# Recurrent attention and a feed-forward layer on one core: token pairs for the logits, sums on row halves, and another order of work

## Chip, cores and metric

The kernel runs on one core of a Trainium2 chip. The metric is device time in microseconds; the table below gives the runs of the kernel before the change, their median and the one execution that was profiled.

## What is computed

The reference is a gated recurrence over 768 tokens for 4 x 8 heads of width 48, and a feed-forward layer on its output:

```python
f = 1.0 / (1.0 + np.exp(-f_logit))                  # B, H, S, D = 4, 8, 768, 48
for t in range(S):
    state = f[:, :, t, :, None] * state + np.einsum('bhd,bhe->bhde', k[:, :, t], v[:, :, t])
    y[:, :, t] = np.einsum('bhd,bhde->bhe', q[:, :, t], state)
x = y.transpose(0, 2, 1, 3).reshape(B * S, H * D)    # 3072 x 384
h = x @ w_in                                         # 384 x 2048
out = (h * (1.0 / (1.0 + np.exp(-h)))) @ w_out       # 2048 x 384
```

Inputs and output are float32 in DRAM; the matmuls work on bf16 operands.

## The kernel before

The 768 tokens of each of the 4 batches are cut into 6 chunks of 128. A work item is a pair of two chunks, and `PAIRS` lists 12. Pairs 0 to 3 (form T) hold chunks 0 and 1 of one batch, with two neighbouring tokens in one partition, so their loads read 384 bytes in one run (two tokens of 48 floats). Pairs 4 to 11 (form N) hold the same chunk of two batches, one token per partition, so their loads read 192 bytes in one run.

For each pair the logits `f` become softplus values `lf` on ScalarE (`E` an Exp, line 312, `L` a Ln, lines 324 and 327). TensorE sums them over the tokens with a triangular matrix (`cs`, lines 388 and 395), and gives in a few columns more the total of a chunk (lines 392 and 398). ScalarE takes Exp of the sums (`a`, `ia`, `al`, lines 400, 402, 342). VectorE and GpSimd multiply q and k with them (`qg`, `ki`, line 405). q and k are turned either on TensorE with a copy out of PSUM (`tq`, line 412, `qkc`) or by a DMA transpose on SP's queue (`qkD`, line 424). Then come the scores (`sc`, lines 434 and 438, on the array's row halves because a head has 48 rows), the mask (`at`, line 442), y (`y`, `yi`, lines 349, 455, 459), the state (`d`, `sd`, `su`, lines 361, 476, 480, 490), and y turned into `xT` (`yT` on TensorE, line 467, with a copy `xc`, or `yD` by DMA, line 471).

The feed-forward layer works per pair in 8 tiles of hidden columns: `mi` (line 335, x times w_in, six matmuls of 256 columns, or two halves of 128 columns for pairs 0 and 1), `si` (line 340, Silu on ScalarE). The second product takes the plain form for pairs 0, 1 and 11 (`mo`, line 370) and for the others one that saves an eighth of the multiplications by summing halves of the hidden values (`hs`, line 256) and of w_out (`wt`, line 246) on VectorE: seven products `ms` (line 273), combined by `cc`, `ca` and `oc` before the store `so`.

The order on every engine is written out by hand in the table `PLAN`. A word such as `cs.4.1:P:3` names the operation, the pair and half, the engine (P TensorE, A ScalarE, V VectorE, G GpSimd, S SP's DMA queue) and the buffer it takes. Each engine runs its words in the order of the table and waits by semaphore for what they need. Loads of q, k, v and f go through SP's queue. The weights go through GpSimd's queue (`wi`, line 237, `wo`, line 240), which casts them to bf16 on the way, so their issue stands in line with GpSimd's products. `idle` (line 545) issues matmuls on a cleared tile, whose result nobody reads. ScalarE changes its function table (line 593) whenever it goes from Exp and Ln to Silu or back.

Of the kernel before, what the change touches and what calls it, by code (L numbers as in the profile page):

```python
# [11 lines left out]
BF16 = mybir.dt.bfloat16  # L12
AF = mybir.ActivationFunctionType
ALU = mybir.AluOpType
# [23 lines left out]
PLAN = """  # L38
f.1.0:S:0 k.1.0:S:0 f.0.0:S:1 f.0.1:S: q.1.0:S:0 f.2.0:S:2 E.1.0:A: L.1.0:A:0 v.1.0:S:0 cs.1.0:P:0 E.0.0:A: q.0.0:S:1 L.0.0:A:1 idle.512.1::1
cs.1.1:P:1 a.1.0:A:0 E.0.1:A: k.0.0:S:1 qg.1.0:V:0 L.0.1:A: a.1.1:A:1 f.3.0:S:0 ia.1.1:A:2 idle.512.2::2 cs.0.0:P:2 qg.1.1:V:1 ia.1.0:A:3 ki.1.1:G:  # L40
cs.0.1:P:3 al.1:A:0 E.2.0:A: q.2.0:S:2 ki.1.0:V: ia.0.0:A:4 tq.1.0:P:4 vb.1.0:V:0 a.0.0:A:0 v.0.0:S:1 vb.1.1:A:1 qkc.1.0:V:0 qg.0.0:G:2 a.0.1:A:1
d.1:P:5,6 L.2.0:A:2 k.2.0:S:2 tq.1.1:P:7 su.1.0:V:0 qg.0.1:G:3 qkc.1.1:A: cs.2.0:P:0 ki.0.0:V: k.3.0:S:3 wi.3:G: sd.1.1:V:0 ia.0.1:A:2 sc.1.0:P:1,2
# [12 lines left out]
mo.1.0.2:P: vb.3.1:V:2 q.4.1:S:4 sd.2.1:V:1 yi.2.1:P: sc.3.1:P:3,6 yc.2.1:V:2 su.2.1:G:0 q.4.0:S: sc.3.0:P:7,4 mo.0.0.3:P: E.4.0:A: at.3.0.0:V:0
k.5.0:S:0 mo.1.0.3:P: at.3.1.0:V:1 L.4.0:A:1 yT.2.0:P:5 at.3.1.1:V: yT.2.1:P:7 v.4.0:S:4 mo.1.1.3:P: xc.2.1:A:2 at.3.0.1:V: oc.1.0:A:0 cs.4.1:P:3
v.5.0:S:0 cs.4.0:P:6 xc.2.0:V: oc.1.1:A: oc.0.0:V:1 d.3:P:7,4 a.4.1:A:1 y.3:P:0,5 q.5.0:S:0 su.3.0:V:0 al.4.1:A:4 ia.4.0:A:4 qg.4.1:G:3 mi.2.7:P:2
E.5.0:A: yc.3.0:V:0 v.6.1:S:1 mi.2.3:P:1 ia.4.1:A:2 sd.3.1:V:0 al.4.0:A:5 yi.3.1:P: a.4.0:A:3 yT.3.0:P:7 f.7.0:S:0 mi.2.1:P:0 su.3.1:G:0 L.5.0:A:2
xc.3.0:V:3 yc.3.1:V:1 mi.2.4:P:3 v.4.1:S: wt.4:V: yT.3.1:P:4 cs.5.0:P:6 mi.2.0:P:7 xc.3.1:V: ki.4.1:V: mi.2.5:P:5 si.2.0:A:2 vb.4.0:V:3 qkD.4.1:S:0
ki.4.0:V:0 mi.2.2:P:4 si.2.7:A: qg.4.0:V: si.2.1:A: mi.3.7:P:7 wt.3:V: si.2.5:A: mi.3.2:P:2 qkD.4.0:S:1 si.2.4:A: si.3.7:A:3 d.4.0:P:0 mi.2.6:P:5  # L60
si.2.3:A: mi.3.1:P:3 si.2.6:A: mi.3.4:P:7 si.2.2:A: vb.5.0:A:0 mi.3.0:P:1 hs.2.1:V:2 q.6.0:S:1 si.3.2:A: vb.4.1:G:1 mo.0.1.0:P:5 si.3.4:A: k.7.0:S:1
wt.1:V: si.3.0:A: mi.3.5:P:4 sd.4.0:V:1 mi.3.6:P:2 f.6.0:S:1 si.3.5:A: wt.7:V: ms.2.3:P:7 si.3.6:A: q.5.1:S: hs.2.5:V:1 mi.3.3:P:1 si.3.1:A: d.4.1:P:0
cs.5.1:P:4 si.3.3:A: ms.2.4:P: sd.4.1:V:0 hs.2.7:V: k.6.1:S:2 sc.4.0:P:2,3 sc.4.1:P:1,0 at.4.0.0:V:2 mo.0.1.1:P: k.5.1:S: a.5.0:A:0 at.4.1.1:V:3
al.5.0:A:1 mo.0.1.2:P: al.5.1:A:0 ia.5.1:A:1 qg.5.0:G:4 at.4.1.0:V: q.6.1:S: ia.5.0:A:2 ms.3.3:P:2 E.7.0:A: cc.2:V:0 ki.5.0:G: at.4.0.1:V: y.4.1:P:0
f.8.0:S:2 L.7.0:A:0 ms.3.4:P: hs.2.6:V: yc.4.1:A:2 tq.5.0:P:6 k.6.0:S: a.5.1:A:4 y.4.0:P:1 qkc.5.0:V:3 E.6.0:A: mo.0.1.3:P: su.4.0:G:0 ca.2.0:V:
yT.4.1:P:3 yc.4.0:A:0 sc.5.0:P:0,4 v.6.0:S: L.6.0:A:1 su.4.1:G:0 d.5.0:P:6 ms.2.2:P: sd.5.0:V:1 q.7.0:S:2 yT.4.0:P:1 xc.4.1:V:0 qg.5.1:G:1 ms.2.5:P:
# [47 lines left out]
def kernel(  # L114
# [10 lines left out]
    nc = tc.nc  # L125
# [369 lines left out]
    def takes(kind, rest):  # L495
# [22 lines left out]
        if kind == "al":  # L518
            return [("al", *rest)]
# [107 lines left out]
```

## Time and profile before

| what | value |
| --- | --- |
| median of 3 runs | 177.3 us (176.36 to 177.46) |
| profiled execution, its own time | 175.56 us |
| its span, first to last instruction | 173.4 us |
| TensorE matmul busy | 160.4 us, 92% |
| ScalarE / VectorE / GpSimd busy | 75% / 70% / 41% |
| bytes moved by DMA | 31.73 MB, mean 183 GB/s |
| DMA packets | 108695, of which 102704 under 512 B |
| ScalarE table loads | 13 in the body, 16.7 us |

The profile is that of one execution. Its page gives busy time per engine, the span in 40 slices, the DMA queues, the chain of work that ended last, and the costliest groups of instructions by line; the trace behind it can be asked for stretches of time, single engines and single transfers. PE is TensorE's matmuls, PEld its weight loads, DVE VectorE, ACT ScalarE, POOL GpSimd, SP the engine that issues most DMAs (SPq and POOLq are the issues). A busy TensorE need not be at its peak, since ends of matmuls overlap, and idle time of an engine that nobody waits for costs nothing.

### The profile page before, as it was taken

To read this page: it belongs to the slowest core of one execution; us is meant where nothing else is said; L and a number is where in the kernel's file an instruction comes from. 1 tells how busy PE (TensorE), PEld (TensorE's weight loads), DVE (VectorE), ACT (ScalarE), POOL (GpSimd) and SP (SyncE) were. 2 spreads that over 40 slices of the span, in tenths; PEclk is the share of its full clock that TensorE was granted. 3 is DMA by queue.
4 is the path that set the end of the run, shared out by engine and by line. 5 is a ranking of instruction groups with operands and counts; after the bars stand their busy time and mean duration, and the time that the engine had idled before them with its cause. 6 is when DMAs were issued, how large, how long until landed. Compare 5 with 4: busy or idle time off the path is not lost.

```text
span 173.4 us, 5477 instructions
## 1 busy us (share of the span) xinstructions
PE 160.4 (92%) x2245; PEld 141.5 (82%) x2245; DVE 121.3 (70%) x234; ACT 129.6 (75%) x248; POOL 71.2 (41%) x115
## 2 busy tenths in 40 slices
PE   0687898999999999999999999999996999999993
PEld 0255698976789888999998999999895998999992
DVE  7188950039995997958899779989965677966050
ACT  3999697783989899999768798798955877603511
POOL 6059872930240147899946305202467201000300
PEclk9999999999999999999999999999999999999999
DMA  5999999999999999979999969896999795120305
GB/s 138 324 325 319 241 206 227 203 206 195 185 194 200 195 200 204 176 150 208 245 188 188 219 135 211 191 198 134 191 171 183 177 145 139 60 80 4 136 27 200
DMA packets 108695, 31.73 MB, mean 183 GB/s; under 512 B 102704, under 2 KB 108144, under 8 KB 108672
## 3 DMA queue, kind: packets, MB, share of 16 engines
q1 hardware_dynamic: 103936, 25.70, 71.7%
q0 software_dynamic: 4736, 5.70, 15.8%
q8 instruction: 17, 0.28, 0.6%
q14 instruction: 6, 0.05, 0.1%
HBM read 25.17 MB, written 4.72 MB: 172 GB/s over the span
## 4 chain that ended last, share of the span: by engine, by line
PE 69%; DMA 17%; POOL 4%; SPq 4%; ACT 3%; issue 1%; POOLq 0%
PE pb L335 28%; PE pb L273 22%; PE pb L370 7%; DMA w_in_sb<-in_moe_w_in_dram 6%; DMA w_out_sb<-in_moe_w_out_dram 5%; DMA qkT<-qk 4%; POOL qk L405 3%; DMA f<-in_f_logit_dram 2%; PE pb L438 2%; SPq L305 2%; PE pb L459 2%; PE pb L455 2%; PE pb L395 2%; SPq L424 1%; ACT x L400 1%
## 5 line engine op out<-in xcount | busy, mean ns | idle before, releaser
L335 PE MATMUL pb<-xT,w_in_sb 128*128 128x256 bf16 (+1 forms) x672 | 69.7, 257 | 0.5 <-DMA w_in_sb<-in_moe_w_in_dram 0.5
L340 ACT ACTIVATE hT<-pb 128x512 bf16<-128x512 f32 x96 | 51.9, 605 | 14.1 <-PE pb L335 13.4
L335 PEld LDWEIGHTS <-w_in_sb 128*128 128x128 bf16 x672 | 56.3, 98 | 5.9 <-DMA w_in_sb<-in_moe_w_in_dram 0.6
L273 PE MATMUL pb<-w_sum,hT 128*128 128x192 bf16 x288 | 28.0, 246 | 0.0
L405 POOL TENSOR_TENSOR qk<-q,x 128x384 bf16<-128x384 f32 x16 | 16.3, 1020 | 27.5 <-ACT x L400 12.4
L490 POOL TENSOR_TENSOR st<-sd,al 48x192 bf16<-48x192 f32 x32 | 16.9, 529 | 25.6 <-DVE sd L480 13.5
L400 ACT ACTIVATE x<-pb 128x384 f32<-128x384 f32 x48 | 22.2, 511 | 3.3 <-PE pb L395 2.7
L273 PEld LDWEIGHTS <-hT 128*128 128x128 bf16 x288 | 23.8, 98 | 0.6
L442 DVE TENSOR_TENSOR atm<-pb,triu 128x512 bf16<-128x512 f32 x32 | 20.5, 683 | 5.2 <-PE pb L438 5.0
L370 PE MATMUL pb<-w_out_sb,hT 128*128 128x384 bf16 (+1 forms) x128 | 17.7, 286 | 0.1
L593 ACT ACT_TABLE_LOAD x13 | 16.7, 1283 | 0.2
L405 POOL TENSOR_TENSOR qk<-k,x 128x384 bf16<-128x384 f32 x13 | 13.8, 1062 | 6.7 <-ACT x L400 5.4
L273 PE MATMUL pb<-w_out_sb,qkTT 128*128 128x192 bf16 x144 | 14.7, 246 | 0.0
L256 DVE TENSOR_TENSOR hT<-hT 128x1024 bf16<-128x1024 bf16 x18 | 14.6, 813 | 0.0
L382 POOL DMA_DIRECT2D out_dram<-ob x7 | 3.9, 565 | 24.6 <-ACT hT L340 24.6
L370 PEld LDWEIGHTS <-hT 128*128 128x128 bf16 x128 | 11.1, 98 | 3.6 <-issue 0.3
L191 ACT CAST yb<-pb 128x384 bf16<-128x384 f32 x15 | 7.3, 490 | 8.5 <-PE pb L349 4.8
L312 ACT ACTIVATE f<-f 128x768 f32<-128x768 f32 (+1 forms) x13 | 10.4, 809 | 2.4 <-DMA f<-in_f_logit_dram 2.2
L273 PEld LDWEIGHTS <-qkTT 128*128 128x128 bf16 x144 | 12.0, 98 | 0.3
L256 DVE TENSOR_TENSOR qkTT<-hT 128x2048 bf16<-128x2048 bf16 x9 | 11.1, 1233 | 1.2 <-ACT hT L340 1.2
L193 DVE COPY qkTT<-pb 128x1024 bf16<-128x1024 bf16 x4 | 2.8, 692 | 12.0 <-PE pb L412 12.0
L442 DVE TENSOR_TENSOR atm<-pb,mask 128x512 bf16<-128x512 f32 x16 | 10.0, 684 | 1.3 <-PE pb L434 1.3
(86 smaller groups left out, 235.6 us busy)
## 6 DMA issues: line engine op xcount, KB each, us to landing
f<-in_f_logit_dram SPq DMA_DIRECT2D x11, 384.0 KB, 4.8
k<-in_k_dram SPq DMA_DIRECT2D x16, 192.0 KB, 4.1
q<-in_q_dram SPq DMA_DIRECT2D x16, 192.0 KB, 3.7
v<-in_v_dram SPq DMA_DIRECT2D x16, 192.0 KB, 4.1
k<-in_k_dram SPq DMA_DIRECT2D x4, 384.0 KB, 4.9
q<-in_q_dram SPq DMA_DIRECT2D x4, 384.0 KB, 4.8
v<-in_v_dram SPq DMA_DIRECT2D x4, 384.0 KB, 10.7
w_in_sb<-in_moe_w_in_dram POOLq DMA_DIRECT2D x4, 384.0 KB, 8.8
```

The source lines that it names most:

```text
L191: nc.scalar.copy(dst, src)
L256: return ENG[eng].tensor_tensor(out=h_sum(P, m), in0=x, in1=y, op=op)
L273: nc.tensor.matmul(at(BANK[m], P)[:, half * W:(half + 1) * W], x, w, start=first, stop=(n == KH - 1), skip_group_check=True)
L312: return nc.scalar.activation(e, at("f", P)[:, j * w:(j + 1) * w], AF.Exp, scale=-1.0)
L335: nc.tensor.matmul(h[:, i, cols], w_in_sb[:, kk, n * 128:(n + 1) * 128], at("xT", P)[:, kk, cols], start=(kk == 0), stop=(kk == KT - 1))
L340: return nc.scalar.activation(at("hT", P).rearrange("p u n c -> p n u c")[:, 2 * j:2 * j + 2], at("h", P, j).rearrange("p (n u c) -> p n u ...
L370: nc.tensor.matmul(at("o", P, i)[:, cols], at("hT", P)[:, i, n], w_out_sb[:, n, cols], start=(n == 0), stop=(n == NT - 1))
L400: nc.scalar.activation(at(kind, P, i).rearrange("p h d -> p (h d)"), at("cs", P, i)[:, 0:HD], AF.Exp, scale=1.0 if kind == "ia" else -1.0)
L405: ENG[eng].tensor_mul(at("qk", P, i)[:, j, :, 0:D], heads("qk"[j], P, i), at("ia" if j else "a", P, i))
L442: ENG[eng].tensor_mul(at("atm", P, i)[:, r], at(f"s{r}", P, i).rearrange("p (n c) -> p n c", c=C), mask[:, None, :].to_broadcast([C, NP, C]))
L490: ENG[eng].tensor_mul(at("st", P, i)[lo:lo + D, :, r * D:(r + 1) * D], src[lo:lo + D, :, r * D:(r + 1) * D], al_of(P, i)[lo:lo + D, :, Non ...
L593: nc.scalar.preload_act_table_set(TABLES[mode])
```

## The change

Four things change. First, the logits of pairs 4 to 11 come as two neighbouring tokens per partition: each batch's chunk fills 64 partitions, in a DMA of its own with runs of 384 bytes. Second, their sums are made by one word `cs` per pair: for each parity of the token and each half of the partitions one matmul of 64 rows, with two new triangular masks `tpair`, and column sums on 64 rows likewise. Third, pair 0's logits come in one transfer with one Exp and one Ln instead of two. Fourth, `idle` reads the triangular mask repeated four times instead of a cleared tile, there are 7 such matmuls instead of 3, and the whole table has a new order: pair 0 goes ahead of pair 1, w_out is issued later, y of five more halves is turned by DMA (15 instead of 10 in form N), q and k of two halves fewer (12 instead of 14). The diff, without the table:

```diff
-    zero = sb.tile([C, 512], BF16, name="zero")
     two = any(kind == "T" for kind, *_ in PAIRS)
+    merged = {int(w.split(":")[0].split(".")[1]) for w in PLAN.split() if w.startswith("cs.") and w.split(":")[0].count(".") == 1}
+    if merged:
+        tpair = [sb.tile([C, C], BF16, name=f"tpair{j}") for j in range(2)]
...
-            if T:
+            if kind == "f" and P in merged:
+                for r in range(2):
+                    nc.sync.dma_start(out=at("f", P)[r * HC:(r + 1) * HC].rearrange("p (h w) -> p h w", h=H),
+                                      in_=f_logit[b + r, :, c * C:(c + 1) * C].rearrange("h (p t) d -> p h (t d)", t=2))
+                return
+            elif T:
...
-                if T:
+                if T or P in merged:
...
-            if T:
+            if T or P in merged:
...
+        if kind == "cs" and len(rest) == 1:
+            lf = at("lf", P)
+            for j in range(2):
+                for r in range(2):
+                    rows = slice(r * HC, (r + 1) * HC)
+                    nc.tensor.matmul(at("cs", P, r)[:, 0:HD].rearrange("p (h d) -> p h d", d=D), tpair[j][rows], lf[rows, j, :, 0:D], start=(j == 0), stop=(j == 1), skip_group_check=True)
+            if us[0][1] < CHUNKS - 1:
+                for j in range(2):
+                    for p in range(NP):
+                        for r in range(2):
+                            rows = slice(r * HC, (r + 1) * HC)
+                            nc.tensor.matmul(at("cs", P, r)[:, HD + p:HD + p + 1], lf[rows, j, 2 * p:2 * p + 2, :], ones[rows], start=False, stop=(j == 1), skip_group_check=True)
+            return
...
+        if kind == "cs" and len(rest) == 1:
+            return [(kind, P, i) for i in range(2)]
...
-                nc.tensor.matmul(buf["pb", int(got)][:, 0:rest[0]], triu, zero[:, 0:rest[0]], start=True, stop=True, skip_group_check=True)
+                nc.tensor.matmul(buf["pb", int(got)].rearrange("p (n c) -> p n c", c=C), triu, triu[:, None, :].to_broadcast([C, 4, C]), start=True, stop=True, skip_group_check=True)
...
-        nc.vector.memset(zero, 0.0)
...
+        if merged:
+            for j in range(2):
+                nc.gpsimd.memset(tpair[j], 0.0)
+                for r in range(2):
+                    half = tpair[j][r * HC:(r + 1) * HC]
+                    nc.gpsimd.affine_select(out=half, in_=half, compare_op=ALU.is_gt, fill=1.0, base=j, pattern=[[-1, C]], channel_multiplier=2)
```

Three places show how the table moves work. In each row stand the line, the operation, the tile written and the tiles read. The first place is TensorE's queue at the sums: before, pair 4's two halves stand between a product of `mo` and the state of pair 3.

```order
L395 MATMUL pb_135<-lf_80,triu 128x384
L398 LDWEIGHTS lf_80
L398 MATMUL pb_135<-ones,lf_80 128x1
...
L395 MATMUL pb_138<-lf_80,triu 128x384
...
L361 MATMUL pb_139<-vb_98,qk_89 128x96
```

Now, for pair 5, whose sums stand between the scores of pair 4's two halves (line 457, the old 438):

```order
L457 MATMUL pb_139<-qkT_99 128x128
...
L375 MATMUL pb_138<-lf_81,tpair_149 128x384
L375 LDWEIGHTS tpair_149
L375 MATMUL pb_136<-lf_81,tpair_149 128x384
...
L375 MATMUL pb_136<-lf_81,tpair_150 128x384
L381 LDWEIGHTS lf_81
L381 MATMUL pb_138<-ones,lf_81 128x1
...
L457 MATMUL pb_133<-qkT_100 128x128
```

What moved: two matmuls of 384 columns on full rows are four on row halves, in two PSUM banks in turn, and the sums now have scores, which are on row halves too, on both sides; for the other pairs of form N scores or other products on row halves stand on at least one side of the sums, or next to the sums of the pair beside them.

The second place is GpSimd's queue around the second weights. Before, they are issued after the state updates of pairs 0 and 1, between products of q and k (`qk`) of pair 3:

```order
L490 TENSOR_TENSOR st_140<-sd_122,al_124 48x4x48 x2
L490 TENSOR_TENSOR st_141<-sd_121,al_123 48x4x48 x2
L240 DMA w_out_sb<-in_moe_w_out_dram 128x4x384 x2
L405 TENSOR_TENSOR qk_88<-q_72,x_86 128x8x48
L405 TENSOR_TENSOR qk_89<-q_72,x_84 128x8x48
L240 DMA w_out_sb<-in_moe_w_out_dram 128x4x384
L405 TENSOR_TENSOR qk_89<-k_67,x_85 128x8x48
L240 DMA w_out_sb<-in_moe_w_out_dram 128x4x384
```

Now:

```order
L238 DMA w_in_sb<-in_moe_w_in_dram 128x3x512
L194 CAST vb_96<-v_76 128x384
L424 TENSOR_TENSOR qk_88<-k_67,x_86 128x8x48
L424 TENSOR_TENSOR qk_89<-q_72,x_83 128x8x48
L509 TENSOR_TENSOR st_142<-sd_122,al_124 48x4x48 x2
L194 CAST vb_98<-v_78 128x384
L509 TENSOR_TENSOR st_141<-sd_121,al_125 48x4x48 x2
L194 CAST vb_92<-v_77 128x384
L194 CAST vb_93<-v_77 128x384
L241 DMA w_out_sb<-in_moe_w_out_dram 128x4x384 x2
L194 CAST vb_94<-v_78 128x384
L241 DMA w_out_sb<-in_moe_w_out_dram 128x4x384 x2
```

What moved: the four issues of w_out stand behind the last issue of w_in, pair 3's products, the state updates of pairs 2 and 1 (`st_142`, `st_141`), and casts of the values of pairs 4 and 3.

The third place is ScalarE's queue at the first Silus (`hT`). Before, sixteen of them stand in one row after one table load. Now:

```order
L346 ACTIVATE hT_118<-pb_133 128x2x2x128
L346 ACTIVATE hT_118<-pb_138 128x2x2x128
L619 ACT_TABLE_LOAD
L318 ACTIVATE f_62<-f_62 128x768
L330 ACTIVATE lf_79<-f_62 128x8x2x48
L619 ACT_TABLE_LOAD
L346 ACTIVATE hT_117<-pb_134 128x2x2x128
L346 ACTIVATE hT_117<-pb_132 128x2x2x128
```

What moved: Exp and Ln of pair 4's logits, which stood behind the sixteen, now stand behind the ninth, with a table load on either side.

More of the change, by code (lines that the diff above doesn't have):

```diff
@@ L38 @@
 PLAN = """
[L39 to L42, printed above, removed]
@@ L107 @@
-mo.11.1.1.0:P: oc.10:V: mo.11.0.2.0:P: ca.10.3:V: mo.11.0.3.0:P: mo.11.1.2.0:P: oc.11.0.0:V:2 mo.11.1.3.0:P: so.11.0.0:S: mo.11.1.0.1:P:
-mo.11.1.1.1:P: so.8.1:S: mo.11.0.0.1:P: so.10.0:S: oc.11.1.0:V: mo.11.0.1.1:P: so.11.1.0:S: mo.11.0.2.1:P: so.10.1:S: mo.11.0.3.1:P: mo.11.1.2.1:P:
-oc.11.0.1:A: mo.11.1.3.1:P: so.11.0.1:S: oc.11.1.1:A: so.11.1.1:S:
+f.1.0:S:0 f.0.0:S:1 f.2.0:S:2 v.0.0:S:0 q.0.0:S:0 E.1.0:A: L.1.0:A:0 k.0.0:S:0 E.0.0:A: idle.512.2::0 cs.1.1:P:0 q.1.0:S:1 L.0.0:A:1 E.2.0:A:
+idle.512.1::1 cs.0.1:P:1 f.3.0:S:0 vb.0.1:G:0 L.2.0:A:2 vb.0.0:G:1 cs.0.0:P:2 ia.1.1:A:0 k.1.0:S:1 a.0.0:A:1 ia.0.0:A:2 qg.0.0:V:0 idle.512.2::3
@@ new lines @@
+cs.1.0:P:3 v.1.0:S:1 a.0.1:A:3 ki.0.0:V: ia.0.1:A:4 qg.0.1:V:1 al.0:A:0 idle.512.1::4 tq.0.0:P:4 ia.1.0:A:1 k.2.0:S:2 ki.0.1:V: a.1.1:A:2 tq.0.1:P:5
+a.1.0:A:3 qkc.0.0:V:0 qg.1.1:G:2 d.0:P:6,7 q.2.0:S:2 qkc.0.1:A: cs.2.0:P:2 su.0.0:V:0 qg.1.0:G:3 E.3.0:A: sc.0.1:P:1,3 v.2.0:S:2 sd.0.1:V:0 cs.2.1:P:4
+wi.1:G: L.3.0:A:1 at.0.1.0:V:0 sc.0.0:P:5,6 at.0.1.1:V: ki.1.1:G: k.3.0:S:3 al.2:A:1 a.2.0:A:4 cs.3.1:P:7 ia.2.0:A:2 at.0.0.1:V:1 cs.3.0:P:1 ki.1.0:G:
+ia.2.1:A:3 tq.1.1:P:3 at.0.0.0:V: q.3.0:S:3 al.1:A:2 a.2.1:A:0 idle.512.1::2 tq.1.0:P:2 qkc.1.1:A:1 wi.2:G: y.0:P:6,0 qkc.1.0:V: vb.1.0:G:2 yi.0.1:P:
@@ new lines @@
+si.11.2:A: mi.11.5:P:1 si.11.0:A: si.11.4:A: ms.10.6:P:6 si.11.7:A: mo.11.1.0.0:P:5 si.11.6:A: mo.11.1.1.0:P: si.11.5:A: ms.10.5:P: mo.11.1.2.0:P:
+mo.11.0.0.0:P:0 mo.11.1.3.0:P: mo.11.0.1.0:P: oc.11.1.0:A:1 mo.11.0.2.0:P: so.11.1.0:S: ms.10.2:P: so.9.1:S: ms.10.1:P:2 oc.10:V:2 mo.11.0.3.0:P:
+ca.10.1:V: mo.11.0.0.1:P: ca.10.2:V: ms.10.7:P: oc.11.0.0:V: mo.11.1.0.1:P: ca.10.3:V: mo.11.0.1.1:P: mo.11.1.1.1:P: so.10.1:S: mo.11.1.2.1:P:
+so.11.0.0:S: mo.11.1.3.1:P: so.10.0:S: mo.11.0.2.1:P: oc.11.1.1:V: mo.11.0.3.1:P: so.11.1.1:S: oc.11.0.1:A: so.11.0.1:S:
```

124 lines of the change are left out of this document (60 added, 64 removed).

## The prediction

> **What bounds the kernel now.** I read the page first, then the busy time by stretches, then the chain of waits and the timelines of single engines.
>
> ```profile
> span 173.4 us, 5477 instructions
> PE 160.4 (92%) x2245; PEld 141.5 (82%) x2245; DVE 121.3 (70%) x234; ACT 129.6 (75%) x248; POOL 71.2 (41%) x115
> ...
> DMA  5999999999999999979999969896999795120305
> ```
>
> TensorE is busy for 92%, nobody else for more than 75%. But the DMA row is full for most of the run too, so two resources have to be followed. The stretches say where TensorE is not full (columns: stretch, its length, then busy time and count of PE, PEld, DVE, ACT, POOL, then the clock, the DMA share and GB/s):
>
> ```profile
> 0.00:6.00 6.00, 0.00 (x0) 0.10 (x1) 3.15 (x25) 2.97 (x3) 2.85 (x18) 1.00 0.71 190
> 6.00:12.00 6.00, 5.59 (x52) 2.95 (x52) 3.16 (x5) 5.85 (x15) 1.35 (x2) 1.00 1.17 325
> 12.00:24.00 12.00, 10.28 (x244) 8.09 (x244) 10.57 (x19) 10.22 (x24) 10.26 (x14) 1.00 1.19 269
> ...
> 60.00:120.00 60.00, 60.00 (x812) 55.00 (x811) 52.41 (x92) 52.11 (x102) 31.36 (x44) 1.00 0.92 189
> 120.00:140.00 20.00, 18.53 (x242) 16.66 (x241) 14.39 (x25) 14.70 (x27) 10.84 (x17) 1.00 1.00 176
> ...
> 160.00:173.40 13.40, 10.55 (x119) 9.98 (x116) 2.76 (x6) 4.20 (x9) 1.61 (x3) 1.00 0.34 119
> ```
>
> Between 60 and 120 us TensorE never rests, although the DMA share is 0.92. So the DMA engines are full without anyone waiting: loads are only early or late within their slack. Losses are at the start (6.0 us with no matmul, then 52 short matmuls in 6 us), 1.5 us in 120 to 140, and 2.9 us at the end, which are the last copy and store. The 1.5 us are one wait for one DMA transpose:
>
> ```profile
> 22.21 0.51 PE L335 MATMUL pb<-xT,w_in_sb 128*128 128x128 bf16 x6
> ...
> 24.84 2.17 PE L335 MATMUL pb<-xT,w_in_sb 128*128 128x128 bf16 x36
> 27.49 7.21 PE L335 MATMUL pb<-xT,w_in_sb 128*128 128x128 bf16 x126 [0.48 <-DMA w_in_sb<-in_moe_w_in_dram]
> ...
> 132.88 0.40 PE L438 MATMUL pb<-qkT 48*128 48x128 bf16 x8 [1.47 <-DMA qkT<-qk]
> ```
>
> The first row of this fence is the first useful feed-forward matmul, at 22.21. What the change can win is therefore in the first 30 us and in that one wait; everywhere else it wins only by taking work off TensorE.
>
> **The change part by part.**
>
> *The start.* Pair 0 now comes before pair 1, and its logits in one transfer. ScalarE's rows:
>
> ```profile
> 4.26 0.84 ACT L312 ACTIVATE f<-f 128x768 f32<-128x768 f32 x1 [2.24 <-DMA f<-in_f_logit_dram]
> 5.14 0.84 ACT L324 ACTIVATE lf<-f 128x768 bf16<-128x768 f32 x1
> ...
> 8.41 1.23 ACT L400 ACTIVATE x<-pb 128x384 f32<-128x384 f32 x3
> ...
> 12.59 1.04 ACT L191 COPY qkTT<-pb 128x1024 bf16<-128x1024 bf16 x1
> ```
>
> An Exp or Ln of 768 columns takes 0.88 from start to start. Now six of them (pairs 1, 0, 2) run before any Exp of sums: 4.26 + 6 x 0.88 = 9.55. The Exps of sums follow at 0.38 each, so the first that pair 0 needs ends at 10.3. The rest of the chain comes from these groups:
>
> ```profile
> L405 DVE TENSOR_TENSOR qk<-k,x 128x384 bf16<-128x384 f32 x11 | 7.8, 709 | 0.2 <-ACT x L400 0.2
> L405 DVE TENSOR_TENSOR qk<-q,x 128x384 bf16<-128x384 f32 x8 | 5.0, 629 | 4.1 <-ACT f L312 3.8 <-ACT x L400 0.4
> L442 DVE TENSOR_TENSOR atm<-pb,mask 128x512 bf16<-128x512 f32 x16 | 10.0, 684 | 1.3 <-PE pb L434 1.3
> L405 POOL TENSOR_TENSOR qk<-k,x 128x384 bf16<-128x384 f32 x13 | 13.8, 1062 | 6.7 <-ACT x L400 5.4 <-POOL st L490 0.7 <-DMA k<-in_k_dram 0.3
> ```
>
> Four products on VectorE, 2 x (0.63 + 0.71) = 2.7, end at 13.0; transposes 0.4; the ScalarE copy 1.05, 14.5; scores 0.6, 15.1; four masks at 0.68, 17.8; y 0.45; ScalarE's cast, one transpose and two copies with three Exps between them, about 3.1. The first feed-forward matmul is ready at 21.4, **0.8 earlier** than now.
>
> *The weights' first half.* GpSimd now issues w_in behind other products:
>
> ```profile
> 13.54 0.95 POOL L237 DMA_DIRECT2D w_in_sb<-in_moe_w_in_dram x1
> ...
> w_in_sb<-in_moe_w_in_dram POOLq DMA_DIRECT2D x1, 384.0 KB, 7.3
> ...
> w_in_sb<-in_moe_w_in_dram POOLq DMA_DIRECT2D x1, 384.0 KB, 10.7
> ```
>
> First issue: pair 1's Exp ends at 12.3, two products of 1.06, so 14.4; landing 7.3 later, 21.7, against 21.4 when it is wanted. Last issue: 14.4 plus three issues of 0.8, five more operations of 0.5 to 1.06 and an update of 1.06, about 23; landing 30.5 (33.7 by the slower row). TensorE wants that quarter after 21 half tiles of 6 x 56 ns (2.17 us for 36 above, ends overlapping) and 3 us of attention: 21.7 + 7.1 + 3.0 = 31.8. Costs nothing, up to 2. VectorE's longer queue (three masks and a product ahead of pair 2's copy) costs about 1.0 near 24.
>
> *ScalarE's detour.* Pair 4's Exp and Ln now stand between Silus of pairs 0 and 1, with a table load on either side:
>
> ```profile
> L593 ACT ACT_TABLE_LOAD x13 | 16.7, 1283 | 0.2
> ```
>
> 2 x 1.28 + 2 x 0.86 = 4.3 us with no Silu. TensorE has 5.5 us of work whose PSUM is free at that point (from 31.4 to 36.9), and the first bank comes back near 37.3: 0.4 lost, up to 2.5 if the logits of pair 4 land late. By these steps pairs 0 and 1 are through their first products at about 38, and pair 2's are done at 46.3. In work done that is **0.6 behind** the present kernel (-0.8 + 1.0 + 0.4; ends -1.5 and +3).
>
> *The sums.* Columns of the chain's rows: start, length, engine and line:
>
> ```profile
> 46.46 0.16 PE pb L395
> 46.62 0.08 PE pb L398 x4
> 46.70 0.18 PE pb L395
> 46.88 0.08 PE pb L398 x4
> 46.96 0.45 PE pb L361 x16
> 47.41 0.40 PE pb L349 x32
> 47.81 1.42 PE pb L335 x12
> ...
> 49.56 1.31 PE pb L335 x12
> ```
>
> Two tokens per partition turn two 128-row matmuls of 384 columns (0.34) into four of 64 rows. The trace has no such matmul, but L361 streams the same 4 x 384 = 1536 columns on row halves, in 0.45: +0.11. The 16 column sums replace eight: +0.05. Eight pairs, the last two without column sums: +1.2; pair 4's share is in the start already, so **+1.1**. Bounds: -0.5 if the halves overlap perfectly, +4 if they don't (0.34 + 0.16 more per pair).
>
> The row pair at the end of that fence speaks against the change: twelve matmuls behind row halves take 1.42, behind full rows 1.31, so leaving row halves costs 0.11. The Trainium skill, "TensorEngine Tiling (Array Packing)", section Key Properties, says that a change of tiling mode drains TensorE; the row agrees in sign. By that rule alone, two changes for each of eight pairs would be 1.8 us. But the changed order puts all eight beside scores or other products that are on row halves already, so I add nothing.
>
> *w_out later.* Here the four issues move:
>
> ```profile
> 24.92 1.55 POOL L240 DMA_DIRECT2D w_out_sb<-in_moe_w_out_dram x2
> ...
> 33.49 0.81 POOL L240 DMA_DIRECT2D w_out_sb<-in_moe_w_out_dram x1
> ...
> w_out_sb<-in_moe_w_out_dram POOLq DMA_DIRECT2D x1, 384.0 KB, 8.5
> ```
>
> In GpSimd's queue they are now behind pair 2's state update, which needs pair 2's y (about 34.5), another update and casts of pairs 3 and 4: first issue at 38.3, last at 42. At 7.5 to landing and 3.1 from one to the next (as w_in: 13.54 + 7.3 to 19.40 + 10.7), they land at 46, 49, 52 and 55. TensorE first reads them at 49.6 (pair 2's products, then five of pair 3's at 0.66) and needs the last at 55.0, the summed weights a microsecond later. No slack: **+0.5**, 0 to +4.
>
> *Loads, transposes, copies.* Logits of pairs 4 to 11 move as 384-byte runs instead of 192: less DMA time, nobody waits for it in 60 to 120. Five turns of y leave TensorE for the DMA (5 x 0.17) and two turns of q and k come back (2 x 0.45): 0. The clearing of a 512-column tile goes; GpSimd builds two masks in about 1.4 us (estimated from its 2.85 us of building in the first stretch), and of 6 to 12 it is busy for only 1.35: 0. Four more warming matmuls run where TensorE is idle anyway: 0.
>
> *The wait at 132.9.* The chain shows the transpose behind it:
>
> ```profile
> 126.29 6.54 DMA qkT<-qk
> ```
>
> Pair 10's first half is now turned some 8 us of matmuls ahead of its scores: **-1.5**; 0 if another transpose is late instead.
>
> Sum: 0.6 + 1.1 + 0.5 - 1.5 = +0.7, a span of 174.1. The profiled execution took 175.56 us in all, 2.2 outside the span and below the three runs shown (176.36 to 177.46, median 177.3). On the median it makes **178.0 us**, +0.4%. About 1% is what a measurement here can tell from no change.
>
> **The rivals.**
>
> *Slower: starved loads.* While weights moved, loads of the SP queue took far longer than the usual 4 to 5:
>
> ```profile
> v<-in_v_dram SPq DMA_DIRECT2D x1, 384.0 KB, 17.7
> ...
> f<-in_f_logit_dram SPq DMA_DIRECT2D x1, 384.0 KB, 19.7
> ```
>
> Today that falls on loads nobody needs before 45. With w_out moving from 38 to 55, it falls on pair 4's transposes (issued near 46.6, wanted by the scores at 59) and on pair 6's logits, behind which ScalarE now holds pair 5's. At 14.5 to 17 us they land at 61 to 64: 2 to 5 us of stall, 3.5 taken, so 181. It decides once the last w_out lands after 55. For it: 0.71 to 1.20 of DMA share. Against: SP itself is held by the first transpose until 46.6, so w_out has the engines nearly alone before.
>
> *Faster: the start wins more.* Nothing but w_in competes with pairs 2 to 4 before 38, so their loads land about 5 us earlier than today, the 1.0 and 0.4 above vanish, 0.8 is won, and w_out is in time: -0.8 + 1.1 - 1.5 = -1.2; with sums that cost nothing and halves that overlap, -2.5: 174.8. For it: 17.7 and 19.7 above. Against: VectorE's queue, not a load, is what I see holding pair 2.
>
> *Slower: row halves do not run together.* +4 instead of +1.1, 181; L361 and L349 speak against it. The drain rule above gives the same sign, 1.8 more, 179.8, if scores beside the sums do not share their mode.
>
> **How the numbers follow.** Forecast 0.38, starved loads 0.24, faster start 0.30, row halves or drains 0.08. The forecast's own range is 176.2 to 179.8. The range over all reaches to 173.8 (the faster case with the start at its low end) and 182.5 (starved loads at the long end). Faster by over 1%: the faster case and a bit of the forecast's low end, 0.32; slower: the two slower cases, 0.32; within 1%: 0.36.
>
> **What would show it.** Right: first feed-forward matmul at 21 to 22; a gap of under 1 us near 37 behind the second table load; a merged sum of about 0.65 with its column sums; no wait on w_out over 1 us; no wait on qkT over 1 us past 100; TensorE full from 60 on. Wrong: TensorE idle between 46 and 62 for w_out, qkT or the sums of pair 5 (starved loads); a merged sum near 0.8 or 1.0 (halves apart); feed-forward matmuls from 20 and pair 2's products done by 45 (faster start).

## The result

The changed kernel took a median of **187.8 us** (four runs, 187.4 to 194.9) against 176.9 for the kernel before on the same chip (176.4 to 177.5): a ratio of **1.065** (95% interval 1.0585 to 1.0711). That is some 11 us slower where 178.0 was forecast, and past the range's end of 182.5. The ratios here and below leave disturbed runs out, while the medians hold all of them; the profiled execution took 194.85 us, so places and causes are read from its trace, and totals from the ratios.

The start of the page of the changed kernel, with the rate in GB/s over 40 slices of the span:

```profile
span 192.7 us, 5635 instructions
PE 169.6 (88%) x2314; PEld 145.6 (76%) x2314; DVE 124.2 (64%) x233; ACT 125.5 (65%) x241; POOL 69.5 (36%) x112
...
GB/s 163 324 325 265 257 217 216 167 182 186 200 14 13 201 213 164 214 136 237 194 150 172 139 131 206 194 98 180 129 223 148 147 116 211 35 110 16 82 65 143
```

Two slices, 53 to 63 us, move 14 and 13 GB/s: something holds the loads' own queue. The stretches (length, busy time and count of PE, PEld, DVE, ACT, POOL, then clock, DMA share, GB/s):

```profile
0.00:6.00 6.00, 1.07 (x3) 0.27 (x4) 3.14 (x24) 3.05 (x4) 4.46 (x24) 1.00 0.72 194
6.00:12.00 6.00, 5.83 (x39) 3.16 (x39) 1.96 (x4) 5.94 (x13) 1.00 (x3) 1.00 1.17 325
12.00:24.00 12.00, 10.96 (x280) 8.56 (x276) 10.91 (x19) 10.43 (x23) 11.31 (x15) 1.00 1.19 274
48.00:60.00 12.00, 7.71 (x52) 5.14 (x51) 9.72 (x9) 6.47 (x12) 6.29 (x5) 0.86 0.50 89
60.00:120.00 60.00, 51.31 (x630) 42.75 (x629) 35.70 (x64) 39.40 (x79) 17.46 (x25) 0.94 0.92 173
120.00:140.00 20.00, 19.98 (x266) 18.56 (x266) 15.55 (x29) 12.34 (x26) 10.97 (x14) 0.91 0.75 152
```

The start is as good as before, and the wait in 120 to 140 is gone. The waits lie in 48 to 120: 4.3 us of TensorE idle by 60, another 8.7 by 120. Behind them, to 140, the granted clock is under 1.00, where the kernel before had 1.00 throughout; TensorE's busy time rises from 160.4 to 169.6 us with it (the same 2314 matmuls take 162.6 in the run "With the stores as well" below, whose trace has 1.00 throughout). So in this execution about half of the extra time is waiting, and much of the rest is matmuls that run slower behind the waits. TensorE's timeline (start, length, line and operation; in brackets the idle time ahead of it and what ended that):

```profile
21.05 1.18 PE L341 MATMUL pb<-xT,w_in_sb 128*128 128x128 bf16 x18 [0.34 <-DMA w_in_sb<-in_moe_w_in_dram]
...
37.19 1.49 PE L341 MATMUL pb<-xT,w_in_sb 128*128 128x128 bf16 x18 [0.91 <-ACT hT L346]
...
41.25 0.50 PE L375 MATMUL pb<-lf,tpair 64*128 64x384 bf16 x4
41.58 0.34 PE L381 MATMUL pb<-ones,lf 64*128 64x1 bf16 x16
41.79 0.50 PE L367 MATMUL pb<-vb,qk 64*128 64x96 bf16 x16
...
49.03 0.81 PE L389 MATMUL pb<-w_out_sb,hT 128*128 128x384 bf16 x4
...
56.76 0.50 PE L495 MATMUL pb<-vb,qk 128*128 128x96 bf16 x4 [4.29 <-POOL qk L424]
57.06 5.34 PE L389 MATMUL pb<-w_out_sb,hT 128*128 128x384 bf16 x24
...
69.28 0.96 PE L375 MATMUL pb<-lf,tpair 64*128 64x384 bf16 x4 [3.93 <-ACT lf L330]
```

Two waits of about 4 us, on GpSimd's product for pair 4 and on pair 5's logits. GpSimd, SP and ScalarE, followed back from them:

```profile
40.77 1.48 POOL L241 DMA_DIRECT2D w_out_sb<-in_moe_w_out_dram  x2
53.55 1.48 POOL L424 TENSOR_TENSOR qk<-q,x 128x384 bf16<-128x384 f32 x1 [11.30 <-DMA q<-in_q_dram]
55.00 1.70 POOL L424 TENSOR_TENSOR qk<-k,x 128x384 bf16<-128x384 f32 x1
56.66 2.67 POOL L509 TENSOR_TENSOR st<-sd,al 48x192 bf16<-48x192 f32 x2
59.41 1.59 POOL L424 TENSOR_TENSOR qk<-q,x 128x384 bf16<-128x384 f32 x1
```

```profile
39.37 1.23 SPq L311 DMA_DIRECT2D q<-in_q_dram  x1
40.70 8.34 SPq L296 DMA_DIRECT2D f<-in_f_logit_dram  x2
61.03 1.33 SPq L443 DMA_TRANSPOSE qkT<-qk  x1
62.47 2.64 SPq L296 DMA_DIRECT2D f<-in_f_logit_dram  x4
```

```profile
53.21 1.28 ACT L619 ACT_TABLE_LOAD   x1
66.78 1.58 ACT L318 ACTIVATE f<-f 128x768 f32<-128x768 f32 x2 [12.29 <-DMA f<-in_f_logit_dram]
68.39 0.84 ACT L330 ACTIVATE lf<-f 128x768 bf16<-128x768 f32 x1
```

```profile
q<-in_q_dram SPq DMA_DIRECT2D x1, 192.0 KB, 14.0
```

Read upwards: one q load of pair 4 is issued at 39.37, between the issues of w_out, and needs 14.0 us (last row), where the median of the sixteen loads of q of this size is 3.9. GpSimd's next product (`qg.4.0`) reads it and waits 11.3 us; behind it stand the two products that make chunk 1 of pair 4. Their turn is SP's next instruction, and it goes out at 61.03 only. Behind that turn stand the logits of pairs 6 and 7, issued at 62.47. ScalarE has pair 6's Exp ahead of pair 5's Ln, so pair 5's sums on TensorE wait until 69.28. By this reading, which the experiments test, one late load has passed through three queues that run in order.

### The profile page after: what moved, and what is told of

It is laid out like the page before. It is cut to its first block, busy times and chain, and to the rows that moved or that the text cites. A ratio compares the mean times of both kernels' runs of the same rounds, so it can differ in the third digit from the quotient of the medians.

```text
span 192.7 us, 5635 instructions
## 1 busy us (share of the span) xinstructions
PE 169.6 (88%) x2314; PEld 145.6 (76%) x2314; DVE 124.2 (64%) x233; ACT 125.5 (65%) x241; POOL 69.5 (36%) x112
## 5 line engine op out<-in xcount | busy, mean ns | idle before, releaser
L341 PE MATMUL pb<-xT,w_in_sb 128*128 128x256 bf16 (+1 forms) x672 | 71.9, 261 | 1.2 <-ACT hT L346 0.9
L346 ACT ACTIVATE hT<-pb 128x512 bf16<-128x512 f32 x96 | 51.0, 613 | 21.8 <-PE pb L341 21.4
L509 POOL TENSOR_TENSOR st<-sd,al 48x192 bf16<-48x192 f32 x32 | 19.5, 609 | 34.7 <-PE pb L474 27.6
L274 PEld LDWEIGHTS <-hT 128*128 128x128 bf16 x288 | 24.2, 99 | 1.1 <-issue 0.3
L318 ACT ACTIVATE f<-f 128x768 f32<-128x768 f32 x12 | 10.1, 847 | 21.6 <-DMA f<-in_f_logit_dram 21.6
L389 PE MATMUL pb<-w_out_sb,hT 128*128 128x384 bf16 (+1 forms) x128 | 20.2, 311 | 0.0
L257 DVE TENSOR_TENSOR qkTT<-hT 128x2048 bf16<-128x2048 bf16 x9 | 12.4, 1373 | 9.3 <-ACT hT L346 9.3
L389 PEld LDWEIGHTS <-hT 128*128 128x128 bf16 x128 | 12.1, 104 | 4.8 <-issue 2.6
L257 DVE TENSOR_TENSOR hT<-hT 128x1024 bf16<-128x1024 bf16 x18 | 12.1, 682 | 0.0
L499 DVE TENSOR_TENSOR sd<-pb,st 128x384 f32<-128x384 f32 x16 | 8.7, 552 | 5.1 <-PE pb L495 2.9
L424 DVE TENSOR_TENSOR qk<-k,x 128x384 bf16<-128x384 f32 x12 | 8.3, 694 | 3.9 <-DMA k<-in_k_dram 3.9
L194 DVE CAST yb<-pb 128x384 bf16<-128x384 f32 x12 | 6.7, 555 | 6.4 <-PE pb L355 2.9
```

The source lines that it names most:

```text
L257: return ENG[eng].tensor_tensor(out=h_sum(P, m), in0=x, in1=y, op=op)
L274: nc.tensor.matmul(at(BANK[m], P)[:, half * W:(half + 1) * W], x, w, start=first, stop=(n == KH - 1), skip_group_check=True)
L318: return nc.scalar.activation(e, at("f", P)[:, j * w:(j + 1) * w], AF.Exp, scale=-1.0)
L341: nc.tensor.matmul(h[:, i, cols], w_in_sb[:, kk, n * 128:(n + 1) * 128], at("xT", P)[:, kk, cols], start=(kk == 0), stop=(kk == KT - 1))
L346: return nc.scalar.activation(at("hT", P).rearrange("p u n c -> p n u c")[:, 2 * j:2 * j + 2], at("h", P, j).rearrange("p (n u c) -> p n u ...
L389: nc.tensor.matmul(at("o", P, i)[:, cols], at("hT", P)[:, i, n], w_out_sb[:, n, cols], start=(n == 0), stop=(n == NT - 1))
```

## The experiments

Theory A: the chain just read is the cost. Rivals: the weights' place in itself (B), the token pairs and row halves (C), the DMA engines' rate (D). Ratios are against the kernel before, run on the same chip. The diffs show the moved words of `PLAN` with a neighbour or two; the words between are left out.

**The changed kernel again.**

> The changed kernel once more, for a profile to compare with. In the first one TensorE waits 4.3 us at 52.5 for GpSimd's product of k of pair 4, and 3.9 us at 65.4 for the sums of pair 5. Queue theory: q of pair 4, first half, is the last load of its pair, is issued at 39.4 in the middle of the w_out issues and lands at 53.4; GpSimd's next product waits for it, everything behind it on GpSimd waits too, then the DMA transpose on SP that needs those products, then the logits of pairs 6 and 7 queued behind the transpose, then ScalarE, which holds pair 5's Ln behind pair 6's Exp. Sums theory: the row halves and the paired tokens cost the time. Bandwidth theory: w_out at 38 to 51 leaves too little transfer rate for pairs 4 to 6, whatever the order. Expected of all: 187 to 188 us, both waits there again, and after each wait a stretch with a lower granted clock.

Measured: 190.5 us (186.8 to 194.4), the same two waits (3.43 up to 55.99, 3.91 up to 68.49). They are the kernel's. Its trace has another of 1.86, up to 124.67, for a turn of pair 7.

**Pair 4's q load early.**

```diff
-xc.2.0:V: q.4.0:S: mi.1.0.0:P:2
+f.4.0:S:1 q.4.0:S:4 yT.0.1:P:0
```

> One load moved: q of pair 4, first half, is issued right behind the logits of pair 4, before the values of pairs 3 and 4, so some 15 us earlier. Queue theory: it lands before 40, GpSimd's product follows at once, the transpose of pair 4 is issued near 46.5 instead of 61, both TensorE waits go, and the time is 177 to 180. Bandwidth theory: the transfer that lands late is then another one (logits of pair 5 or 6, the transposes), the waits move to 58 to 66, and the time is 183 to 187. Sums theory: 187.

Measured: 184.0 us, ratio 1.048 (1.039 to 1.056). Both long waits are gone and the turn is issued at 49.31: A is right about them. They are not all, though: waits of 0.4 to 1.3 us stay between 60 and 116, and ScalarE still waits 2.3 to 4.5 us for logits four times.

**The logits ahead of the turn.**

```diff
-si.3.6:A: f.6.0:S:0 hs.2.5:V:0
-si.3.2:A: f.7.0:S:1 si.3.0:A:
+f.5.0:S:2 f.6.0:S:0 f.7.0:S:1 si.1.1:A:
```

> Only the second link of the chain is cut: the logits of pairs 6 and 7 are issued right behind those of pair 5, ahead of the transpose that waits for GpSimd. Queue theory: the first wait (4.3 us near 52.5) stays, the second (sums of pair 5) goes or shrinks to under 1.5, since ScalarE no longer waits for pair 6's logits; but the scores of pair 4's other half then wait for its transpose, so 3 to 5 us are won: 183 to 185. Bandwidth theory: two more loads in front make the transposes later and the time is 187 to 190.

Measured: 184.4 us, 1.051 (1.042 to 1.059). TensorE's timeline:

```profile
53.20 0.34 PE L495 MATMUL pb<-vb,qk 128*128 128x96 bf16 x4 [1.63 <-POOL qk L424]
...
74.68 0.82 PE L274 MATMUL pb<-w_sum,qkT 128*128 128x192 bf16 x8 [2.50 <-ACT x L419]
```

The second wait is gone, so it did come over SP's queue; the first, expected to stay, shrinks to 1.63 (the q load takes 11.3 here), and a new one stands at 74.

**The new order without the pairs in the sums and loads** (pairs 4 to 11 as before, nothing moved).

```diff
-cs.4:P:4,2
+cs.4.0:P:4 cs.4.1:P:2
```

> The new order is kept, but the logits of pairs 4 to 11 come one token per partition in runs of 192 bytes, and their sums are made on full rows as before. Queue theory: the sums are innocent; the time is 187 to 190, a little slower if anything since the logits take more transfer time. Sums theory: at least 3 us faster, under 185.

Measured: 190.7 us (186.4 to 193.6), as the changed kernel run beside it (186.8 to 194.4); waits of 5.45 up to 57.00 and 2.00 up to 68.51 take the same places. The fastest runs of the two are 186.4 and 186.8: C explains nothing that can be told here, though a microsecond or two would hide in this scatter.

**w_out early.**

```diff
-si.1.1:A: wo.0:G: sc.3.1:P:3,7
+wi.0:G: wo.0:G: wo.2:G: wo.1:G: wo.3:G: qkc.2.1:V:
```

> The changed order with one thing put back: the four w_out issues stand right behind the last w_in issue on GpSimd, at about 23 to 27 instead of 37.6 to 42.2. If w_out's place alone costs the time, the loads of pair 4 and the logits of pairs 6 and 7 come in time, both TensorE waits of 4 us go, and the time is 177 to 180. If the weights hit whatever is in flight, the loads of pairs 3 and 4 are late instead: ScalarE waits for pair 4's logits between its Silus near 34 to 40 and TensorE for its PSUM there, 3 to 5 us, and the time is 181 to 185.

Measured: 188.2 us, 1.073 (1.064 to 1.083). Issued at 23.6, the weights hit another load. TensorE, then ScalarE:

```profile
43.13 2.72 PE L341 MATMUL pb<-xT,w_in_sb 128*128 128x128 bf16 x18 [5.57 <-ACT hT L346]
```

```profile
39.45 0.84 ACT L318 ACTIVATE f<-f 128x768 f32<-128x768 f32 x1 [5.65 <-DMA f<-in_f_logit_dram]
```

Now pair 4's logits are late, with the Silus behind them. B falls as it was put: the weights' old neighbourhood costs as much in this order, and both times a load beside the weights is late and something stands behind its reader.

**The late product behind the ones it held up.** The load stays late; only GpSimd's order changes.

```diff
-sd.3.1:V:1 qg.4.0:G:3 mi.2.0:P:4
+qg.4.1:G: qg.4.0:G: mi.3.2:P:5
```

> No transfer is moved. On GpSimd alone, the product that waits for the late load (q of pair 4, first half) goes behind the three operations that it held up. Queue theory: those run near 43 to 46, the transpose goes out at about 46 instead of 61, the late load still lands near 53, and the first wait (4.3 us at 52.5) is gone; 182 to 185, as in the run that moved the load (184.0). If the late load itself is what costs, because its own scores wait: 187 to 190.

Measured: 182.7 us, 1.044 (1.035 to 1.053). GpSimd, then TensorE:

```profile
44.50 0.99 POOL L424 TENSOR_TENSOR qk<-k,x 128x384 bf16<-128x384 f32 x1 [2.90 <-ACT x L419]
...
46.93 1.00 POOL L424 TENSOR_TENSOR qk<-q,x 128x384 bf16<-128x384 f32 x1
52.06 1.15 POOL L424 TENSOR_TENSOR qk<-q,x 128x384 bf16<-128x384 f32 x1 [4.13 <-DMA q<-in_q_dram]
```

```profile
51.84 4.06 PE L389 MATMUL pb<-w_out_sb,hT 128*128 128x384 bf16 x24
...
102.00 0.82 PE L274 MATMUL pb<-w_sum,hT 128*128 128x192 bf16 x8 [1.06 <-ACT hT L346]
...
114.17 0.40 PE L457 MATMUL pb<-qkT 48*128 48x128 bf16 x8 [1.52 <-DMA qkT<-qk]
```

The q load lands as late as before, at 52, and costs nothing: the two products that the turn needs are done at 47.9, and SP issues it at 47.95 instead of 61.03. That shows the first cause: not the slow load but its place at the head of a queue. 4.4% are left.

**All late logits moved up**, on top of the early q load and with f.6 and f.7 behind f.5 as above.

```diff
-al.5.1:A:0 f.8.0:S:2 al.5.0:A:1
+k.6.1:S:1 f.8.0:S:2 mo.0.1.1:P:
-mi.4.4:P:3 f.10.0:S:1 sd.5.1:V:1
+f.9.0:S:0 f.10.0:S:1 vb.5.1:A:4
-si.6.0:A: f.11.0:S:2 mi.6.5:P:1
+so.0.0:S: f.11.0:S:2 mi.5.5:P:7
```

> On top of q of pair 4 early (184.0): the logits of pairs 6 and 7 ahead of the waiting transpose, those of pair 8 right behind the first k of pair 6, those of pair 10 behind pair 9's and ahead of two turns of y, those of pair 11 ahead of k of pair 8. In the run with q early ScalarE still waited for logits four times (2.8, 2.8, 2.3 and 4.5 us), and with it TensorE in pieces of 0.5 to 1.4 us between 59 and 117. If SP's order is the cause of those too, most of them go and the time is 178 to 181. If transfer rate is the cause, other loads are late instead and it stays at 182 to 185.

Measured: 185.0 us, 1.055 (1.045 to 1.065), no better than the early q load alone. Of ScalarE's waits for logits one of 2.35 is left, others come (GpSimd waits 5.46 us for a k). This order of SP's queue only chose another load to be late.

**The old order with token pairs** (pairs 4, 5, 6 and 9; for pair 6 one Exp of sums goes behind them).

```diff
-cs.4.1:P:3
-cs.4.0:P:6
+cs.4:P:6,3
```

> The order before the change, with the new form of the logits and sums for pairs 4, 5, 6 and 9 alone (w_out, loads and everything else where they were; the warming matmuls read the mask). If the form is innocent: within 1% of the kernel before, 175 to 178. If row halves and half-width transfers cost: 178 or more.

Measured: 176.2 us against 175.5, 1.006 (1.002 to 1.010). Four of the eight pairs in the new form cost about 1 us (0.4 to 1.7), so C is far too small for the loss; all eight were not run in the old order.

**The stores back on GpSimd.** The changed order also moves six output stores of pairs 0 to 4 from GpSimd's queue to SP's, and one the other way. In the stretch 50 to 125 the transfers (queue, count, size, median us to landing) are, before:

```profile
out_dram<-ob POOLq DMA_DIRECT2D x10, 96.0 KB, 3.8
out_dram<-ob SPq DMA_DIRECT2D x4, 96.0 KB, 3.0
```

and in the changed order with the product mended:

```profile
f<-in_f_logit_dram SPq DMA_DIRECT2D x12, 192.0 KB, 4.0
...
out_dram<-ob SPq DMA_DIRECT2D x12, 96.0 KB, 2.3
```

The edit, on top of the mended product, for all eight stores of these pairs on SP; two of them (`so.0.1`, `so.4.0`) were on SP in the old order too, so it goes a little further than back:

```diff
-so.1.0:S: so.0.1:S: so.0.0:S: so.2.0:S: so.2.1:S: so.3.1:S: so.4.0:S: so.4.1:S:
+so.1.0:G: so.0.1:G: so.0.0:G: so.2.0:G: so.2.1:G: so.3.1:G: so.4.0:G: so.4.1:G:
```

> The changed kernel with pair 4's first product behind its second on GpSimd (182.7 us), and now the eight output stores that SP issued between 74 and 107 us (twelve issues of 0.63 us) on GpSimd instead, at the same places of the order. Theory that SP's own issue time paces the loads after 50 us (SP issues for 73 of 81 us there, in the kernel before 75 of 81 with fewer stores): loads move up by up to 7 us late in that stretch, ScalarE's waits for logits past 85 shrink, 178 to 181 us. Theory that the DMA engines' rate paces them (share 0.86 to 0.92): nothing is moved less, 182 to 183.5. If GpSimd, now waiting for output copies, holds the products behind them, slower than 183.5.

Measured: 177.7 us, **1.006** (1.001 to 1.010); the medians of all runs, 177.7 and 175.75, give 1.011. Most of the rest of the loss is gone. SP's timeline without the edit, and with it (an execution of 179.7 us):

```profile
54.45 1.75 SPq L443 DMA_TRANSPOSE qkT<-qk  x1
...
73.98 1.22 SPq L399 DMA_DIRECT2D out_dram<-ob  x2
...
95.43 2.50 SPq L399 DMA_DIRECT2D out_dram<-ob  x4
...
102.91 1.23 SPq L399 DMA_DIRECT2D out_dram<-ob  x2
...
104.83 2.62 SPq L399 DMA_DIRECT2D out_dram<-ob  x4
107.49 1.38 SPq L296 DMA_DIRECT2D f<-in_f_logit_dram  x2
```

```profile
55.42 1.80 SPq L443 DMA_TRANSPOSE qkT<-qk  x1
...
103.29 1.58 SPq L296 DMA_DIRECT2D f<-in_f_logit_dram  x2
```

The same turn goes out 1.0 later in the second kernel, the same load of logits 4.2 **earlier**: the twelve store issues of some 0.63 us between are missing. And the engines carry more:

```profile
96.00:108.00 12.00, 10.49 (x120) 9.12 (x118) 8.11 (x15) 8.73 (x17) 1.39 (x2) 1.00 0.86 180
```

```profile
96.00:108.00 12.00, 9.48 (x113) 8.38 (x111) 7.97 (x15) 7.28 (x15) 5.08 (x10) 1.00 1.17 212
```

The share rises from 0.86 to 1.17 (1.00 is no ceiling of this column: 1.19 stands in 12 to 24 above); TensorE itself is full from 108 on only. So D falls for this part: the engines had room, and it was SP that issued the loads too late.

**The Exps of logits later on ScalarE**, on top of the mended product.

```diff
-q.5.0:S:0 E.6.0:A: hs.3.5:V:1
+cc.2:A:0 E.6.0:A: L.6.0:A:1
```

(E.7.0 and E.8.0 likewise.)

> The changed kernel with pair 4's first product behind its second on GpSimd (182.7 us), and the Exps of the logits of pairs 6, 7 and 8 right ahead of their own Ln on ScalarE, behind the earlier pairs' Exps and copies. Theory that a late load costs because ScalarE stands at its Exp with an earlier pair's work behind it: the waits of 0.4 to 1.3 us on x and lf between 60 and 92 go, 180 to 181.5. Theory that the pair whose logits are late is itself what TensorE needs next: no change, 182 to 183.5.

Measured: 183.0 us, 1.038 (1.031 to 1.045), against 1.044 without it: no gain that can be told. ScalarE's order was not the cost. **With the stores as well:**

> The edits of the two kernels before this one together, on top of pair 4's product moved. If both theories hold and add, 176 to 179.5; if the DMA engines' rate and the order of use are what is left, 182 to 183.5.

Measured: 178.5 us, 1.011 (1.005 to 1.017), no different from the stores without it.

**The control: the old order with stores on SP.**

```diff
-so.0.0:G: so.1.1:G: so.1.0:G: so.2.0:G: so.2.1:G: so.4.1:G: so.3.1:G:
+so.0.0:S: so.1.1:S: so.1.0:S: so.2.0:S: so.2.1:S: so.4.1:S: so.3.1:S:
```

> The kernel before with the seven output stores that GpSimd issues up to 107 us on SP instead (eleven issues of 0.6 us), nothing else changed. Theory that SP's issue time paces the loads: the old order's loads have slack, but some 6 us less of it, 177 to 180 us. Theory that SP's time does not matter: within 0.5 of the kernel before.

Measured: 177.2 us against 175.75, 1.007 (1.002 to 1.012). Slower, with the expected sign and less than 2 us.

**The stores alone**, pair 4's product left in its place.

> The changed kernel with only the eight output stores of SP before 107 us on GpSimd; pair 4's first product stays at the head of GpSimd's queue. If the two causes add: the waits of about 4 us at 52 and 65 stand, the 5 us of the stores are won, 182 to 184. If the stores cost only because the waits had used up the slack (or the waits only because of the stores), one of the two is won whole or nothing: below 180 or above 186.

Measured: 184.9 us, 1.042 (1.033 to 1.050). The two long waits stand (3.43 and 4.88). (The median of all four runs is 1.052 times that of the kernel before.) From 1.065 each mending alone wins about 2.2 points, both together 5.9: they add, and perhaps a bit more, since each ratio has a margin of up to 0.9.

**The old order with fewer stores on SP** (five issues).

```diff
-so.3.0:S: so.4.0:S: so.0.1:S:
+so.3.0:G: so.4.0:G: so.0.1:G:
```

> The kernel before with its five store issues of SP before 113 us on GpSimd as well (the reverse of the run with seven stores moved to SP, which cost 1.3 us). If SP's issue time paces the old order too, 0.5 to 1 us faster than the kernel before; if its loads have slack there, within 0.5.

Measured: 174.8 us against 175.8, **0.993** (0.990 to 0.996): a little faster than both kernels. The one wait of the old profile past 30 us, 1.47 for a turn at 132.9, is not in its trace, where no wait of TensorE between 44 and 160 is over 0.31. This is the old order's counterpart to the run with eight stores on GpSimd: beside it, that one's 1.006 is 1.3% slower (1.006 / 0.993, an estimate over two chips).

**The early q load with the stores** (and the later Exps).

> The other mending of the late product (pair 4's first q load right behind its logits on SP, 184.0 us alone), with the stores on GpSimd and the later Exps. If head-of-queue wait and SP's store issues are the two causes however the first is mended: 176.5 to 179.5. If the move behind the second product did something else besides: above 181.

Measured: 178.1 us, 1.013 (1.008 to 1.019), where the early q load alone had 1.048. The two causes hold however the first is mended.

## Why the prediction was wrong

- *The start (+0.6).* Right: 21.05 for the first feed-forward matmul (21.4 said), 49.03 for the first read of w_out (49.6), a gap of 0.91 at 37 (0.4 said, under 1).
- *The sums (+1.1).* Too dear on TensorE: from 41.25 to 41.79 a pair takes 0.54, against 0.50 before and 0.65 said. The form as a whole, loads and all, was bounded for four pairs only (1.006 in the old order). The rival of row halves falls with the 0.54, and no drain between tile modes is seen there: the sums start at 41.25 behind matmuls on full rows that end at 41.31. The faster start did not come either (21.05, not 20); its -2.5 was no sum of its terms, which make -2.3 with the sums at nothing and -2.8 at their lower bound.
- *The wait at 132.9 (-1.5).* Right about pair 10, whose turn nobody waits for. The term held only in part: TensorE is full from 120 to 180 in the first trace of the changed kernel, but in the second it waits 1.86 for a turn of pair 7 at 124.67, the case that the prediction priced at 0. In the run with the product behind the ones it held up it waits 1.52 for one at 114.17; with the stores on GpSimd as well it waits for none there.
- **w_out later (+0.5): the step that failed first.** It asked only when the weights land and who reads them; that part came true (the last lands at 53.0, 55 said), and no second product waits for them. The price fell on the load beside them. The rival of starved loads named the neighbourhood (46 to 62, turns, pair 5's sums, ScalarE), though as turns and logits that land late themselves, and was argued down with "SP itself is held by the first transpose until 46.6, so w_out has the engines nearly alone before". But SP issued pair 4's q at 39.37, between two issues of w_out, and pair 5's logits from 40.70, both ahead of that transpose in its queue; and that q stood at the head of GpSimd's queue, ahead of the very product that the turn waits for. The rival's price, 3.5 us, was one stall; the chain gave two, 8.2 us together. Mending this alone takes the ratio from 1.065 to 1.044; with the stores mended too it is worth 3.6 points (1.042 to 1.006).
- **Loads, transposes, copies (0): the step that failed next.** It counted the loads' runs and the turns' cost on TensorE, and left out that stores of the first pairs move from GpSimd to SP. Nor did it price the issues of a queue: a load of logits for one pair in two issues instead of one, turns in its way. The reading "the DMA engines are full without anyone waiting: loads are only early or late within their slack" was true of the old order and taken for a property of the kernel. What slack there was lay in SP's issues: the control loses 0.7% with eleven more issues there, and the old order gains 0.7% with five fewer. In the new order with the product mended, the stores are worth 3.8 points (1.044 to 1.006), or 3.0 by the medians of all runs (1.041 to 1.011).

The Trainium skill, "DMA: Bandwidth & Descriptors", section Rules for kernel authors, says that spreading DMAs over SP, ScalarE and GpSimd brings no bandwidth, since all use the same 16 DMA engines, and that it only saves issue time of the sequencer. The runs agree with the rule, with the weight on its last clause: that "only" was 3 to 4% here.

With both causes mended the new order stands at 1.006 (1.001 to 1.010), and some 1.3% above the old order with its stores on GpSimd too. The sum had said +0.4%: the two terms it missed are most of the error, and up to 1% stays without an account. Which of the waits behind 60 belongs to which of the stores was not taken apart, and an order that moves the y turns off SP was not tried.

## What to carry to other kernels

When weights or other bulk move in time, list the loads in flight beside them, and for each the operation that reads it and everything behind that operation in its engine's queue; a late load cost nothing here behind other work, and two stalls at the head of a queue that a DMA queue waited for. Count the issues on a load queue as work of its own (here 0.6 us and more each): stores put there are paid by the loads behind them, though the DMA engines have room (0.86 here) and SP shows as busy in no column. A slack seen in one order of work need not be there in another.

## What the hardware showed beside this

A wait can cost more than its own length. The 24 matmuls of 384 columns behind the wait at 56.76 take 5.34 us; without the wait, in the kernel with the product moved, the same 24 take 4.06; behind the wait of 3.43 in the kernel with the stores alone they take 4.06 too. With w_out early, 18 matmuls of 128 columns take 2.72 behind a wait of 5.57, against 1.49 in the changed kernel behind one of 0.91. The granted clock is 0.86 in 48 to 60 and 0.94 in 60 to 120, where the kernel before has 1.00. In stretches of 2 us it is a fall to half: 0.50 in 102 to 104 of the changed kernel, and 0.50 in 116 to 118 of the kernel with the product moved.

The Trainium skill, "TensorE: Matmul & The Clock Gate", part on the HAM clock gate, has the clock halved after an idle window of about 3.4 us. The rows agree about the half, not about the length: the first of these falls stands behind a wait of 2.14 (up to 100.55), the second behind one of 1.52 (up to 114.17), while none stands behind that wait of 3.43, up to 56.06, or behind the one of 2.50 at 74.68 with the logits ahead. What decides it is not shown. The mean clock goes with the scatter of the changed kernel's runs (0.965 in the one of 194.9 us, 0.980 to 0.990 in the three of 187.4 to 187.9), but which of the two makes the other was not tested.
